# A linear-attention, routed-expert and gated-layer kernel: first routing group of four tiles, first expert's low halves on POOL, other steps per tile

## The chip, the core and the metric

The kernel runs on one NeuronCore of one Trainium2 chip. The metric is the device time of one execution, in microseconds. Three runs of the kernel before gave 971.5, 974.32 and 974.56 us, so its median is 974.32 us. The other rows and figures come from one further execution, taken with the hardware profiler.

## The reference

Three layers stand one behind the other, all in fp32, on 2304 tokens of width 512.

```
kv  = einsum('bhsd,bhse->bhde', k, v);  o = einsum('bhsd,bhde->bhse', q, kv)
x   = o / sqrt(mean(o*o) + 1e-6) * g_norm          # 4 batches, 8 heads, 576 x 64
l   = x @ w_gate + log1p(exp(x @ w_noise)) * noise # 8 experts, the two largest taken
out[mask] += weight * (maximum(x[mask] @ w1[e], 0) @ w2[e])   # 512 -> 1024 -> 512
y   = (1 / (1 + exp(-(out @ m2_gate))) * (out @ m2_val)) @ m2_out  # 512 -> 1536 -> 512
```

## The kernel before, in words

**Stages.** Attention works on 18 tiles of 128 tokens (`for t in range(NT)`, from L1307). Each tile is transposed (`q_transpose`: PE `pqT`, ACT `qT`), multiplied (`attend`: PE `po`) and read out by ACT in three instructions (`oraw`, `sq`, `Lr`), and DVE sums the squares (`ssq`). Between the tiles PE forms the products of keys and values of the next batch (`kv_a`, `kv_b`, `kv_c`: `pkv`, `pkvT`, `pgw`, and DVE's copies `kvbd`).

**Routing.** The tiles are routed in four groups (`GROUPS`). `route(g)` is a generator; each `yield` ends one step, and `advance(n)` moves all open groups n steps on. Its steps give, in this order: the norm (`rms_a`, `rms_y`), the normed logits (`Lr`, `lg`, `sp`, `nl`), the two largest experts (`m`, `oh`, `km`, `mk`), the rank of each token within its expert (PE's `prk` over `mk`, then `ohr`, `ri`, `sb`, `rm`), marks of the rank (`ohv`, L511: for group 0 all on POOL, for groups 1 and 2 half of them, for group 3 none) and the weights of the two experts. After groups 0 and 1, `list_first` makes PE sum the marks (`pfirst`); DVE writes the token numbers `lsa`, and POOL gathers the first two blocks of 128 rows for the first expert. After group 3 the same is done for all lists (`plist`, `lsb`), and POOL gathers the other three blocks.

**Experts.** A product is made in split precision: each operand is a high part and a low part, and three matmuls take high by high, low by high and high by low. `work()` splits one piece of a weight: a piece of `w1` (128x1024) is scaled by `gcol`, ACT writes the high half (L616) and DVE the low half (L617); for `w2` these are L619 and L620. Pieces of the last layer's weights pass through `work()` too. `scale` multiplies gathered rows by their norm (`xs`), `expert_in` transposes them on PE (`pxT`) and splits them (`xh` on ACT, `xl` on DVE). The first expert is done in two passes: `h_first(fp, 0)` for the 256 rows of the first two blocks, with fp = 0 to 3, 24 matmuls each, into `ha`; then `y_step` for the two blocks; then `h_first(fp, 1)` for the other 368 rows into `hh` and `hl`. In the trace `w_0h` to `w_3h` and `w_0l` to `w_3l` are the halves of piece fp; `w1` and `w2` carry the same names there.

**What sets the order.** SP and POOL issue in the order in which the program is written; ACT does so through attention and the first expert's first pass. PE and, until that pass, DVE are ordered by a scheduler that builds the program; where `in_order("DVE")` stands, DVE too keeps the written order. Within the first expert's second pass (L1400 on), the written order of each f is: `h_first` where f is odd, `pump` (splits of the next expert's weights), then POOL's gathers and scalings for expert 1 (L1415 to L1420).

## Time and profile before

| what | before |
|---|---|
| median of three runs | 974.32 us |
| lowest, highest | 971.5, 974.56 us |
| the profiled execution's own time | 973.39 us |
| its span in the trace | 971.6 us |
| PE busy | 930.7 us (96%) |
| DVE, ACT, POOL busy | 615.1, 420.2, 304.0 us |

The span runs from the first to the last instruction of the program; 1.8 us of the execution lie around it. PE's busy time is made of pipelined matmuls whose ends are modelled, so what PE waits for is read from the waits and the gaps and not from the 96%. All starts below count from the span's start.

### The profile page before, as it was taken

What the parts mean: (1) busy time and instruction counts of PE and PEld (TensorE: products, weight loads), DVE (VectorE), ACT (ScalarE), POOL (GpSimd) and SP (SyncE); (2) the same over time, 40 slices, a digit from 0 to 9 for tenths busy, and PEclk for the clock granted to TensorE, in tenths of its full rate; (3) what the DMA queues carried; (4) which work ended last, traced back from release to release, by engine and by line L of the source; (5) the groups of instructions that cost most, each with busy time, mean ns of one, the idle gap of its engine ahead of it and who ended that gap; (6) DMA issues with size and microseconds to landing.
All of it is one profiled execution on the core that took longest, in us unless ns stands there. A gap on an engine that the chain in (4) does not pass through costs nothing.

```text
span 971.6 us, 13989 instructions
## 1 busy us (share of the span) xinstructions
PE 930.7 (96%) x5207; PEld 811.4 (84%) x5207; DVE 615.1 (63%) x1017; ACT 420.2 (43%) x679; POOL 304.0 (31%) x299
## 2 busy tenths in 40 slices
PE   5997989999999999999999998999999999999998
PEld 5986779889898988989898897878788888888886
DVE  1398677858577585828732587676859888813221
ACT  1673443434343343333433676665655554403221
POOL 2141577171364728162201477760000000000000
PEclk8998999999999999999999999999999999999999
DMA  9984596868557465644701565655455747616451
GB/s 273 285 263 168 179 309 209 288 216 298 184 164 248 144 211 186 204 126 142 248 11 53 168 194 165 192 184 169 143 183 185 234 156 220 181 52 198 122 139 44
DMA packets 130441, 178.25 MB, mean 183 GB/s; under 512 B 18496, under 2 KB 76352, under 8 KB 130368
## 3 DMA queue, kind: packets, MB, share of 16 engines
q1 hardware_dynamic: 118608, 154.91, 49.7%
q0 software_dynamic: 8432, 20.26, 7.6%
q10 hardware_dynamic: 3328, 2.13, 0.7%
q8 instruction: 42, 0.69, 0.3%
q14 instruction: 31, 0.25, 0.1%
HBM read 123.12 MB, written 54.15 MB: 182 GB/s over the span
## 4 chain that ended last, share of the span: by engine, by line
PE 60%; DVE 6%; DMA 2%; ACT 2%; issue 2%; POOL 0%; ACTq 0%; DVEq 0%; POOLq 0%
PE pout L1252 15%; PE py L780 14%; PE pga L1154 11%; PE ph L736 10%; PE pgc L1154 6%; PE pgb L1154 3%; DMA raw<-in_moe_w_val_dram 1%; DVE hl L742 1%; DVE wt L978 1%; DVE xf L1052 1%; PE pgv L1122 1%; DMA yg<-ybuf,slot 1%; DVE raw L593 1%; DMA gbuf<-q 0%; DMA ybuf<-yo 0%
## 5 line engine op out<-in xcount | busy, mean ns | idle before, releaser
L677 POOL DMA_INDIRECT xg<-xbuf,lsq x132 | 141.1, 1069 | 149.0 <-DVE xT L723 100.4
L742 DVE SCALAR_TENSOR_TENSOR hl<-ph,hh 128x624 fp32r<-128x624 f32 (+1 forms) x60 | 48.7, 812 | 78.9 <-ACT hh L741 76.7
L741 ACT ACTIVATE hh<-ph 128x624 fp32r<-128x624 f32 (+1 forms) x60 | 41.7, 695 | 104.5 <-PE ph L736 99.4
L978 DVE TENSOR_TENSOR wt<-lw,wt 128x512 fp32r<-128x512 f32 x84 | 57.5, 687 | 31.8 <-ACT wt L977 31.6
L677 POOL DMA_INDIRECT yg<-ybuf,slq x64 | 69.3, 1083 | 19.5 <-issue 18.3
L785 ACT ACTIVATE yo<-py 128x512 f32<-128x512 f32 (+1 forms) x40 | 23.7, 593 | 72.3 <-PE py L780 48.4
L977 ACT ACTIVATE wt<-lw 128x512 fp32r<-128x512 f32 x84 | 50.4, 621 | 1.6 <-issue 1.6
L696 POOL TENSOR_TENSOR xg<-xg 128x512 f32<-128x512 f32 x33 | 37.7, 1145 | 39.8 <-DMA xg<-xbuf,lsq 34.5
L727 DVE TENSOR_TENSOR xl<-xT,xh 128x512 fp32r<-128x512 f32 (+3 forms) x40 | 24.8, 631 | 37.1 <-ACT xh L726 37.1
L1261 DVE COPY oo<-pout 128x512 f32<-128x512 f32 x9 | 6.2, 692 | 66.0 <-ACT oo L1263 53.1
L726 ACT ACTIVATE xh<-xT 128x512 fp32r<-128x512 f32 (+3 forms) x40 | 21.1, 543 | 53.3 <-DVE xT L723 53.3
L1168 ACT ACTIVATE q<-pga 128x1024 f32<-128x1024 f32 x24 | 24.6, 1025 | 42.1 <-PE pga L1154 39.1
L736 PE MATMUL ph<-xh,w_3h 128*128 128x312 f32 (+2 forms) x128 | 39.4, 308 | 3.5 <-DVE hl L742 3.5
L736 PE MATMUL ph<-xh,w_2h 128*128 128x312 f32 (+2 forms) x128 | 39.6, 310 | 3.3 <-DVE hl L742 3.3
L736 PE MATMUL ph<-xl,w_0h 128*128 128x312 f32 (+2 forms) x128 | 40.3, 315 | 1.8 <-DVE xl L727 1.8
L736 PE MATMUL ph<-xh,w_0h 128*128 128x312 f32 (+2 forms) x128 | 40.3, 315 | 0.7 <-ACT xh L726 0.6
L736 PE MATMUL ph<-xh,w_0l 128*128 128x312 f32 (+2 forms) x128 | 40.1, 313 | 0.3 <-PEq L815 0.3
L677 POOL DMA_INDIRECT yg<-ybuf,slot x20 | 19.6, 980 | 64.8 <-issue 53.9
L736 PE MATMUL ph<-xh,w_3l 128*128 128x312 f32 (+2 forms) x128 | 39.3, 307 | 0.0
L736 PE MATMUL ph<-xh,w_1h 128*128 128x312 f32 (+2 forms) x128 | 39.3, 307 | 0.0
L736 PE MATMUL ph<-xh,w_2l 128*128 128x312 f32 (+2 forms) x128 | 39.2, 306 | 0.1
L736 PE MATMUL ph<-xh,w_1l 128*128 128x312 f32 (+2 forms) x128 | 39.1, 306 | 0.0
(1260 smaller groups left out, 2978.8 us busy)
## 6 DMA issues: line engine op xcount, KB each, us to landing
raw<-in_moe_w_dram SPq DMA_DIRECT2D x60, 512.0 KB, 4.9
lw<-wbuf SPq DMA_DIRECT2D x84, 256.0 KB, 4.4
gr<-gbuf SPq DMA_DIRECT2D x18, 512.0 KB, 5.9
ybuf<-yo SPq DMA_DIRECT2D x32, 256.0 KB, 3.3
ybuf<-zero SPq DMA_DIRECT2D x29, 256.0 KB, 6.0
raw<-in_moe_w_gate_dram SPq DMA_DIRECT2D x12, 512.0 KB, 5.3
raw<-in_moe_w_val_dram SPq DMA_DIRECT2D x12, 512.0 KB, 4.6
gbuf<-qv SPq DMA_DIRECT2D x12, 512.0 KB, 3.1
```

What stands on the lines that cost most here:

```text
L677: nc.gpsimd.indirect_dma_start(out=x, out_offset=None, in_=src, in_offset=bass.IndirectOffsetOnAxis(ap=ix, axis=0))
L696: eng.tensor_mul(xv, xv, x[:, :, 128:, None].to_broadcast([128, 4, KD, 32]))
L727: nc.vector.tensor_sub(XL[e, s][:, :, a:z], pt[:, :, o:o + z - a], XA[e, s][:, :, a:z].bitcast(FT))
L736: nc.tensor.matmul(ph, w[:, c, j], x[e, s][:, c, :], start=(n == 0), stop=(n == 3 * KD - 1))
L741: nc.scalar.activation(hh, ph, AF.Relu)
L742: nc.vector.scalar_tensor_tensor(hl, ph, 0.0, hh.bitcast(FT), op0=OP.max, op1=OP.subtract)
L780: nc.tensor.matmul(py[0:m], x[:, f % 2, t], w[:, f % 2, :], start=(n == 0), stop=(n == 3 * FC - 1))
L977: nc.scalar.activation(hi, src, AF.Copy)
L978: nc.vector.tensor_sub(lo, src, hi.bitcast(FT))
L1154: nc.tensor.matmul(ps[:, j, 0:HT[c]], w[:, a, k, s], x[:, k, :], start=(first and i == 0), stop=(i == 5), skip_group_check=not first)
L1168: nc.scalar.activation(q[name], src, AF.Copy)
L1252: nc.tensor.matmul(po, g[x][1][:, f, :], w[:, k], start=(s + f + i == 0), stop=(s == 1 and FCUT + f == FC2 - 1 and i == 2))
```

## The change

It makes the first two routing groups four tiles each (before five and three), gives each tile its own number of routing steps (`STEPS`), and asks for the first lists right behind them. The four `raw` pieces of the first expert's `w1` are multiplied by `gcol` in place on POOL beside tiles 13 and 14, so that ACT's high half is a plain copy, and the low halves of these four and of two of the four `w2` pieces (1 and 3) are written by POOL. The first `w1` piece is split beside tile 15 and no other one inside attention. The first expert's first two blocks are scaled beside tile 16. The warming matmuls in front of the first pass go from four to two. In the second pass `h_first` comes at even f, ahead of that f's `pump`, and POOL scales expert 1's first two blocks ahead of the fourth and fifth block's gathers.

```diff
-GROUPS = [(0, 5), (5, 8), (8, 13), (13, 18)]
+GROUPS = [(0, 4), (4, 8), (8, 13), (13, 18)]
...
-FIRST_SPLIT = 16
+FIRST_SPLIT = 15
+
+STEPS = {3: 6, 4: 4, 5: 4, 6: 3, 7: 3, 8: 3, 9: 3, 10: 3, 11: 3, 12: 3, 13: 3}
...
             if u[0] == "w1":
-                nc.scalar.activation(hi, raw, AF.Copy, scale=gcol)
-                nc.vector.scalar_tensor_tensor(lo, raw, gcol, hi.bitcast(FT), op0=OP.mult, op1=OP.subtract)
+                if u[1]:
+                    nc.scalar.activation(hi, raw, AF.Copy, scale=gcol)
+                    nc.vector.scalar_tensor_tensor(lo, raw, gcol, hi.bitcast(FT), op0=OP.mult, op1=OP.subtract)
+                else:
+                    nc.scalar.activation(hi, raw, AF.Copy)
+                    nc.gpsimd.tensor_sub(lo, raw, hi.bitcast(FT))
             else:
                 nc.scalar.activation(hi, raw, AF.Copy)
-                nc.vector.tensor_sub(lo, raw, hi.bitcast(FT))
+                eng = nc.vector if u[1] or u[2] % 2 == 0 else nc.gpsimd
+                eng.tensor_sub(lo, raw, hi.bitcast(FT))
...
-        advance(1)
         g = group_of[t]
         if t == groups[g][1] - 1:
             routes.append((g, route(g)))
-        if t >= FIRST_SPLIT:
+        advance(STEPS.get(t, 2) - 1)
+        list_first()
+        if FIRST_SPLIT - 2 <= t < FIRST_SPLIT:
+            for x, _ in list(raws)[:2] if t == FIRST_SPLIT - 2 else list(raws)[2:]:
+                nc.gpsimd.tensor_scalar(x, x, gcol, None, op0=OP.mult)
+        if t == FIRST_SPLIT:
             work()
-        list_first()
+        if t == NT - 2:
+            with tc.high_priority():
+                for blk in range(AB):
+                    scale(0, blk, nc.vector)
 
     pw = pa([128, HP * 128], "warm")
-    for _ in range(4):
+    for _ in range(2):
...
-    while not XG:
-        advance(1)
-        list_first()
-    advance(2)
     with in_order("DVE"):
         with tc.high_priority():
             for blk in range(AB):
-                scale(0, blk, nc.vector)
-        advance(1)
-        with tc.high_priority():
-            for blk in range(AB):
                 expert_in(0, blk)
+        work()
         advance(4)
...
-            elif f % 2:
+            elif f % 2 == 0:
                 h_first(f // 2, 1)
...
-                for blk in range(NB - 1) if f == 0 else ():
+                for blk in range(NB - 2) if f == 0 else ():
                     gather(1, blk)
-                if f > 2:
-                    scale(1, f - 3, nc.gpsimd)
+                if f == 1:
+                    scale(1, 0, nc.gpsimd)
+                    scale(1, 1, nc.gpsimd)
+                    gather(1, NB - 2)
+                if f in (3, 5, 7):
+                    scale(1, f // 2 + 1, nc.gpsimd)
```

In the following rows lines count in each kernel's own file, `x4` means four alike in a row, and a name as `w_0_1l` is a weight of expert 0, piece 1, low half (in the trace `w_1l`).

PE in attention, beside tiles 5 to 7. Before, from the transposes of batch 2's products (`pkvT`) on:

```order
L347 MATMUL pkvT<-ident,kvbd_232 128x128 x4
L378 MATMUL pqT<-ident,qp 128x128 x4
L393 MATMUL po<-kvbd_230,qT 128x160 x4
L354 MATMUL pgw<-early,kvT 128x32 x4
L378 MATMUL pqT<-ident,qrem 128x128 x4
L393 MATMUL po<-kvbd_230,qT 128x160 x4
```

With the change, from the product of tile 6 on:

```order
L395 MATMUL po<-kvbd_230,qT 128x160 x4
L471 LDWEIGHTS tri
L471 MATMUL prk<-mk,tri 128x32
L473 LDWEIGHTS ones
L473 MATMUL prk<-mk,ones 128x24
L473 LDWEIGHTS ones
L473 MATMUL prk<-mk,ones 128x16
L473 LDWEIGHTS ones
L473 MATMUL prk<-mk,ones 128x8
L477 LDWEIGHTS ones
L477 MATMUL prk<-before,ones 128x32
L380 MATMUL pqT<-ident,qp 128x128 x4
```

The ranks of group 0 now stand behind tile 6 and ahead of tile 7's transposes; before, they stood behind the transposes of batch 3 (`kvbd_234`), beside tile 11.

ACT at attention's end. Before:

```order
L444 ACTIVATE sp<-lg 128x40
L445 ACTIVATE sp<-sp 128x40
L616 ACTIVATE w_0_0h<-raw,gcol 128x1024
L396 ACTIVATE oraw<-po 128x4x4x32
L399 ACTIVATE sq<-po 128x512
L400 ACTIVATE Lr<-po 128x128
```

With the change:

```order
L446 ACTIVATE sp<-lg 128x40
L447 ACTIVATE sp<-sp 128x40
L398 ACTIVATE oraw<-po 128x4x4x32
L401 ACTIVATE sq<-po 128x512
L402 ACTIVATE Lr<-po 128x128
L622 ACTIVATE w_0_0h<-raw 128x1024
L382 ACTIVATE qT<-pqT 128x512
L398 ACTIVATE oraw<-po 128x4x4x32
L401 ACTIVATE sq<-po 128x512
L402 ACTIVATE Lr<-po 128x128
```

The first weight's high half stood ahead of tile 17's read-out; it now stands ahead of tile 17's `qT` and of the read-outs of tiles 16 and 17.

POOL, from the first marks to expert 1's gathers. Before:

```order
L511 TENSOR_SCALAR ohv<-i_204,rm 128x128 x13
L677 DMA xg<-xbuf,lsa 128x528 x2
L511 TENSOR_SCALAR ohv<-i_204,rm 128x128 x5
L677 DMA xg<-xbuf,lsb 128x528 x5
L677 DMA xg<-xbuf,lsq 128x132 x8
L800 MEMSET zero 128x512
L683 TENSOR_TENSOR xs_0_1641<-xg 128x4x4x32
L677 DMA xg<-xbuf,lsq 128x132 x4
L683 TENSOR_TENSOR xs_1_1655<-xg 128x4x4x32
```

With the change:

```order
L684 DMA xg<-xbuf,lsa 128x528 x2
L1333 TENSOR_SCALAR raw<-raw,gcol 128x1024 x4
L623 TENSOR_TENSOR w_0_0l<-raw,w_0_0h 128x1024
L623 TENSOR_TENSOR w_0_1l<-raw,w_0_1h 128x1024
L513 TENSOR_SCALAR ohv<-i_204,rm 128x128 x5
L623 TENSOR_TENSOR w_0_2l<-raw,w_0_2h 128x1024
L623 TENSOR_TENSOR w_0_3l<-raw,w_0_3h 128x1024
L627 TENSOR_TENSOR w_0_1l<-raw,w_0_1h 128x1024
L627 TENSOR_TENSOR w_0_3l<-raw,w_0_3h 128x1024
L684 DMA xg<-xbuf,lsb 128x528 x5
L684 DMA xg<-xbuf,lsq 128x132 x4
L690 TENSOR_TENSOR xs_0_1592<-xg 128x4x4x32
```

Four scalings and six subtractions now lie between the two sets of gathers, and `xs_0` (with `xs_1` right behind it) comes after four quarter gathers, where it came after eight and `xs_1` after twelve.

The first expert's second pass, DVE. Before:

```order
L617 SCALAR_TENSOR_TENSOR w_1_0l<-raw,gcol,w_1_0h 128x1024
L617 SCALAR_TENSOR_TENSOR w_1_1l<-raw,gcol,w_1_1h 128x1024
L742 SCALAR_TENSOR_TENSOR hl_0_1555<-ph,hh_0_1554 128x2x368
L617 SCALAR_TENSOR_TENSOR w_1_2l<-raw,gcol,w_1_2h 128x1024
L617 SCALAR_TENSOR_TENSOR w_1_3l<-raw,gcol,w_1_3h 128x1024
L620 TENSOR_TENSOR w_1_0l<-raw,w_1_0h 128x1024
L742 SCALAR_TENSOR_TENSOR hl_1_1606<-ph,hh_1_1605 128x2x368
```

With the change:

```order
L749 SCALAR_TENSOR_TENSOR hl_0_1531<-ph,hh_0_1530 128x2x368
L620 SCALAR_TENSOR_TENSOR w_1_0l<-raw,gcol,w_1_0h 128x1024
L620 SCALAR_TENSOR_TENSOR w_1_1l<-raw,gcol,w_1_1h 128x1024
L620 SCALAR_TENSOR_TENSOR w_1_2l<-raw,gcol,w_1_2h 128x1024
L620 SCALAR_TENSOR_TENSOR w_1_3l<-raw,gcol,w_1_3h 128x1024
L749 SCALAR_TENSOR_TENSOR hl_1_1602<-ph,hh_1_1601 128x2x368
```

`hl_0` moved ahead of two weight pieces, `hl_1` ahead of one. On PE, with the change, behind the third piece's matmuls (before, `pxT` stood behind the fourth piece's):

```order
L726 MATMUL pxT<-ident,xs_0_1592 128x128 x4
L726 MATMUL pxT<-ident,xs_1_1594 128x128 x2
L787 MATMUL py<-w_0_0h,hh_0_1530 128x512
L726 MATMUL pxT<-ident,xs_1_1594 128x128
L787 MATMUL py<-w_0_0l,hh_0_1530 128x512
L726 MATMUL pxT<-ident,xs_1_1594 128x128
L787 MATMUL py<-w_0_0h,hl_0_1531 128x512
L787 MATMUL py<-w_0_0h,hh_0_1530 128x512
L743 MATMUL ph<-xh_1_1468,w_0_3h 128x368
L743 MATMUL ph<-xl_1_1469,w_0_3h 128x368
```

Expert 1's first transposes and the first four matmuls of an output block now stand ahead of the fourth piece.

## Rows read from the trace of the kernel before

**Rows 1.** Stretch: us; PE, PEld, DVE, ACT, POOL busy (instructions); PEclk, DMA share, GB/s.

```profile
62.00:82.60 20.60, 12.90 (x91) 9.74 (x91) 18.39 (x78) 12.24 (x31) 7.71 (x11) 0.94 0.53 180
82.60:96.70 14.10, 14.04 (x102) 13.67 (x103) 12.52 (x49) 5.37 (x10) 4.28 (x5) 0.84 0.44 157
112.00:134.20 22.20, 17.22 (x98) 16.01 (x98) 16.14 (x30) 12.30 (x14) 17.44 (x16) 1.00 0.89 287
134.20:153.10 18.90, 18.90 (x80) 15.13 (x81) 14.77 (x19) 6.20 (x11) 13.04 (x13) 0.91 0.77 254
180.00:971.00 791.00, 777.21 (x3997) 672.88 (x3995) 495.13 (x693) 339.04 (x526) 228.82 (x214) 1.00 0.54 171
```

**Rows 2.** PE's waits, 75 to 175 us: total us, times, longest.

```profile
PE prk L469 <- DVE mk L464: 3.5, 1, 3.5
...
PE ph L736 <- DVE xl L727: 1.8, 2, 1.5
```

**Rows 3.** PE's waits, 112 to 135 us.

```profile
PE ph L736 <- DVE hl L742: 2.6, 2, 1.4
PE pxT L719 <- POOL xs L683: 2.0, 1, 2.0
```

**Rows 4.** Timeline in attention: start us, us, engine line op out<-in.

```profile
39.61 0.86 DVE L340 COPY kvbd<-pkv 64x256 f32<-64x256 f32 x2 [3.14 <-PE pkv L337]
...
43.42 1.25 PE L393 MATMUL po<-kvbd,qT 128*128 128x160 f32 x8
...
44.90 0.58 ACT L380 ACTIVATE qT<-pqT 128x512 f32<-128x512 f32 x1
...
46.19 0.20 DVE L428 TENSOR_TENSOR rms_y<-rms_u,rms_y 128x40 f32<-128x40 f32 x1
...
46.48 0.62 ACT L380 ACTIVATE qT<-pqT 128x512 f32<-128x512 f32 x1
...
55.81 0.19 DVE L464 TENSOR_TENSOR mk<-oh 128x40 bf16<-128x40 f32 x1
...
67.86 0.16 DVE L1298 TENSOR_SCALAR lsa<-pfirst 128x2 int32<-128x2 f32 x1 [0.22 <-PE pfirst L1289]
...
72.03 1.13 ACT L616 ACTIVATE w_0h<-raw,gcol 128x1024 fp32r<-128x1024 f32 x1
...
74.03 0.28 ACT L400 ACTIVATE Lr<-po 128x128 f32<-128x128 f32 x1
```

**Rows 5.** Timeline of the first expert's first pass, its input and its end.

```profile
79.11 1.08 ACT L726 ACTIVATE xh<-pxT 128x512 fp32r<-128x512 f32 x2 [3.19 <-PE pxT L719]
...
81.25 1.28 DVE L727 TENSOR_TENSOR xl<-pxT,xh 128x512 fp32r<-128x512 f32 x2
...
82.59 0.58 PE L736 MATMUL ph<-xl,w_0h 128*128 128x256 f32 x1 [1.54 <-DVE xl L727]
...
96.67 0.63 PE L780 MATMUL py<-w_0h,ha 128*128 128x512 f32 x2
```

**Rows 6.** POOL's groups by shape: busy us, mean ns, idle before.

```profile
L511 POOL TENSOR_SCALAR ohv<-i,rm 128x128 f16<-128x128 f16 x18 | 13.4, 762 | 28.4 <-DVE rm L502 16.1 <-DVE oraw L431 12.3
...
L368 POOL COPY qp<-q 128x1024 f32<-128x1024 f32 x6 | 6.2, 1040 | 30.5 <-DMA q<-in_q_dram 29.6 <-PE po L393 0.9
...
L683 POOL TENSOR_TENSOR xs<-xg 128x512 f32<-128x512 f32 x2 | 2.1, 1061 | 0.0
```

**Rows 7.** Timeline: POOL's gathers, and the second pass's first matmul.

```profile
68.31 1.18 POOL L677 DMA_INDIRECT xg<-xbuf,lsa  x1 [0.73 <-DVE oraw L431]
...
100.97 1.76 POOL L677 DMA_INDIRECT xg<-xbuf,lsb  x1 [13.61 <-DVE lsb L1357]
...
112.07 0.43 PE L736 MATMUL ph<-xh,w_0h 128*128 128x368 f32 x1
```

**Rows 8.** The same columns as group 1, behind the wait of 2.0 us.

```profile
134.00:138.00 4.00, 3.81 (x14) 3.09 (x15) 4.00 (x4) 1.19 (x2) 2.14 (x3) 0.61 0.95 325
```

**Rows 9.** DVE's line 617, first piece: ns shortest/median/longest, first and last start.

```profile
L617 DVE SCALAR_TENSOR_TENSOR w_0l<-raw,gcol,w_0h x8: 1277/1280/2389, 73.3 to 469.7; 128x1024 fp32r<-128x1024 f32 x8
```

## The prediction

> **What bounds the kernel now.** I read the table of stages first, then PE's waits, then the timeline where PE waits, since only there can the change give anything. Behind 180 us PE is busy 777 of 791 us [rows 1]: what PE starts earlier there ends earlier, and nothing in that stretch is edited. The gaps lie ahead of it: between 62 and 82.6 us PE is busy 12.9 of 20.6 us, and between 112 and 134.2 us 17.2 of 22.2 [rows 1]. The first is the hand-over from attention to the first expert: PE waits 3.5 us for `mk` of group 2, which stands on DVE behind two weight pieces and two scalings, and 1.8 us for `xl` [rows 2]. The second is the first expert's second pass: 2.6 us for `hl`, 2.0 us for `xs` on POOL [rows 3]. So the sum has three terms: when the first pass starts, how much of that is left when the second pass starts, and how long the second pass takes.
>
> **First pass's start.** Before, it starts in earnest at 82.59 us, with `xl`; attention's last read-out starts at 74.03 and ends at 74.3 [rows 4, 5].
>
> *Attention's end.* Smaller groups let group 0 begin some five microseconds sooner, but the order puts its ranks on PE behind tile 6, which PE has done at 43.42+1.25 = 44.7 us [rows 4]. `mk` must be there first. DVE copies batch 2's `kvbd` ahead of group 0's `rms_y`, and that copy ends at 39.61+0.86 = 40.5 us, bound by PE [rows 4]. From `rms_y` to `mk` group 0 took 55.81+0.19-46.19 = 9.8 us before, mixed with group 1's steps [rows 4]; its own share I put at 5.4, so `mk` comes at 45.9 and PE waits 1.2 us. ACT's next `qT` copies what PE transposes behind that wait, and so comes as late; I carry 2 us into tiles 8 to 12. Bounds: nothing, and 40.5+9.8-44.7 = 5.6 us.
> Group 1 has four tiles instead of three, so its marks are no sooner by much: `lsa` at 66.9 instead of 67.86 [rows 4]. What it queues is new: on DVE group 2's norm stands behind `lsa`, and on ACT tile 14's `qT` behind that norm's `rms_y`, which gets there at 67.7. From there ACT's list is a sum. A tile costs 46.48-44.90 = 1.58 us [rows 4], so four tiles 6.3; `sp` with its wait 0.9; the first weight's high half, now ahead of tile 17, 1.13 [rows 4]; and tile 17's own wait for its product, which follows its `qT`, about 1.2. That is 9.5 us, so attention ends at 77.3, 3 us later than before.
>
> *From there.* The two scalings of rows are on DVE ahead of attention's last sums, so done by 76.3, and the two weight pieces (1.28 us each, [rows 9]) are gone from DVE. What remains is `xh` 1.08 and `xl`, of which one half, 0.64, lies behind the second `xh` [rows 5], and about 0.5 of sums: 77.3+1.1+1.2 = 79.6 us. **The first pass starts 3.0 us earlier.** The bounds are 0 and 6.
>
> **First pass's end: POOL's new queue.** It took 96.67-82.59 = 14.1 us [rows 5]. POOL now supplies the low halves. The nearest rows for a subtraction of 128x1024 are its 128x512 products at 1.06 us, so 2.1 [rows 6]. No row has a scaling of 128x1024: below stands the copy of that size, 1.04, above the marks' rate, 0.76 us for 128 elements and 6.1 for 1024 [rows 6]. I take 1.5: the copy has the same elements and type and is the nearer, and I add what a mark costs beyond 128 elements at the copy's rate, most of it fixed. Both ends go into the range.
> POOL's list: gathers from 66.9, issued by 69.6 (as 68.31 to 70.8 before, [rows 7]); four scalings to 75.6; `w_0l` to 77.7, in time. `w_1l` waits for ACT's `w_1h`, which follows `xh`: 78.4+1.1 = 79.5, so `w_1l` at 81.6; five marks of 0.76 to 85.4; `w_2l` 87.5; `w_3l` 89.6. PE wants `w_2l` at about 87.5 and `w_3l` at 90. So POOL fits with nothing to spare, and the pass ends at 79.6+14.1 = 93.7, or 93.9 with slips, 2.8 us earlier.
>
> **Second pass's start.** POOL is now late for another reason: its five gathers stand behind two more subtractions, of `w2` pieces 1 and 3, and these wait for ACT, which writes `w_1h` only after the last `ha`: 93.9+0.6+1.1 = 95.5. Two subtractions end at 99.7, and the gathers start there instead of at 100.97 [rows 7]. The second pass follows its gathers by 112.07-100.97 = 11.1 us as before. **Left of the 3 us: 1.3.** DVE, freed of two pieces, has `lsb` ready by 98 to 99, so it does not decide.
>
> **The second pass.** `hl_0` no longer stands behind two weight pieces and `hl_1` behind one fewer; and PE has eight transposes and four output matmuls, about 1.8 us, to do between pieces 2 and 3 while `hl_1` is written. So both waits for `hl`, 2.6 us, go [rows 3]. `xs_0` and `xs_1` come after four quarter gathers instead of eight and twelve, so some 13 us sooner by the issue of POOL; the wait of 2.0 us goes too [rows 3]. Right behind that wait the granted clock is 0.61 of full speed over 4 us [rows 8], between the levels of 1.2 and 2.4 GHz; PE had been idle 2 us. Without the wait 4x0.39 = 1.6 us come back. Together 6.2 us. Against it: new short waits of DVE beside POOL, 0.4; and expert 1's last rows, which DVE and ACT must have split some 6 us sooner than before while DVE is busy 14.8 of 18.9 us [rows 1]: 0.5. **5.3 us.** The bounds are 2.6, if only the `hl` waits go, and 6.2.
>
> **Sum.** 1.3+5.3 = 6.6 us. Two fewer warming matmuls cost nothing and give nothing; PE is idle there. Against the profiled execution's 973.4 us (span 971.6 and 1.8 around it) that is 966.8; the median of the three runs is 0.9 above that execution. I forecast **967.2 us**.
>
> **Rivals**, each 0.4 above the sum against the profiled execution, as the forecast is.
> *(a) Attention ends as early as before.* For it: the wait for `mk` on PE rests on an estimate, and the chain behind `lsa` too. Then the pass starts near 76.6, and POOL binds: `w_1l` at 79.8, `w_3l` 87.8, the pass's end 91.5, the gathers 97.5, 3.5 us earlier instead of 1.3: 965.0.
> *(b) POOL and DVE slow each other.* One of line 617's pieces took 2.39 us where the median is 1.28 [rows 9], with POOL's products of 128x512 beside it. The change puts 6.0+12.6+3.8 = 22.4 us of POOL into a stretch in which DVE, busy 12.5 of 14.1 us [rows 1], routes groups 2 and 3. If a fifth is added to POOL's work, 4.5 us, the first pass ends 3 us later than I say, the gathers start at 104, and the loss of 3.2 us leaves 5.3-3.2 = 2.1 us: 971.7. The Trainium skill says the same (GPSIMD Engine Reference, Specifications): GPSIMD's SBUF interfaces are shared with VectorE and contended by DVE instructions with two SBUF inputs. By that rule nearly all of these subtractions would be hit; the one row here bears it out for DVE, and POOL's own products kept close to 1.06.
> *(c) The second pass keeps a wait.* The next expert's weights land late, or `hl_1` still comes after PE: 3 us of the 5.3 stay, 970.2.
> *(d) Slower: POOL's scaling runs at the marks' rate.* Four at 6.1 us end at 94 instead of 75.6; ACT's high half waits for the first, PE's third matmul for `w_0l` at 96, 14 us after its time before; the gathers come at 115. That costs 14.0-5.3 = 8.7 us: 982.5. At 4 us each the gathers come at 106.6, and the loss of 5.6 less 5.3 leaves 974.1: it decides from about 3.9 us a scaling. Against it stand POOL's copy and products, which keep to one or two ns an element; for it, only the marks. The Trainium skill holds a one-input operation on GPSIMD to be roughly at line rate (GPSIMD Engine Reference, Engine selection), which speaks against (d); no row here shows this form.
>
> **Chances.** My forecast 0.42, (a) 0.20, (b) 0.17, (c) 0.13, (d) 0.08. About 0.3%, 2.9 us, is what a measurement of this kernel can tell from no change, so faster means under 971.4 and slower over 977.2. Faster: 0.42+0.20, two thirds of (c) and under half of (b), 0.77. Slower: most of (d) and the tail of (b), 0.07. The rest, 0.16, is no change. The range reaches from 961, a little under what (a) gives with the second pass at its bound and a scaling at the copy's 1.04 (965.0-0.9-1.8 = 962.3), to 974.5, which takes in (b), (c) and the half-way case of (d).
>
> **What the changed profile would show.** Right: PE waiting for `mk` of group 0 near 45 us; ACT's last `Lr` near 77; the first pass's `xl` matmul near 80 and the first output matmul near 94; POOL busy without a break from the gathers to `w_3l` and again up to the second gathers at about 100; no PE wait for `hl` or `xs` in the second pass, and the clock at 1.00 behind it; expert 1 some 7 us earlier than before. Wrong: scalings of over 2 us or subtractions of over 2.6; PE waiting for low halves from POOL for more than 2 us; a second pass that starts no earlier, or still has its gap.

## The result and the profile after

The changed kernel took **984.18 us** (median of 983.37, 983.93, 984.43 and 990.22) against 972.91 us for the kernel before (median of four): the ratio is 1.0129, with a 95% interval of 1.0083 to 1.0175. Forecast were 967.2 us, within 961.0 to 974.5. The profiled execution took 983.37 us, with a span of 981.6.

The same stretches as [rows 1], after (the last one is longer by the 10 us of the span):

```profile
62.00:82.60 20.60, 11.49 (x98) 9.49 (x97) 18.67 (x60) 10.85 (x28) 16.57 (x11) 0.86 0.39 130
82.60:96.70 14.10, 12.02 (x69) 9.95 (x69) 9.86 (x26) 5.30 (x10) 6.77 (x7) 0.72 0.20 61
112.00:134.20 22.20, 17.54 (x90) 14.55 (x90) 12.81 (x31) 3.50 (x6) 11.98 (x10) 0.85 0.45 138
134.20:153.10 18.90, 18.90 (x109) 17.82 (x108) 16.56 (x13) 13.10 (x15) 16.17 (x15) 1.00 0.83 262
180.00:981.00 801.00, 786.12 (x4066) 681.52 (x4065) 506.68 (x709) 342.81 (x530) 233.32 (x218) 1.00 0.54 172
```

POOL is busy 16.57 us in the first stretch where it was 7.71, and PE loses 1.4 there. PE's waits from 75 to 175 us, against [rows 2, 3]:

```profile
PE prk L471 <- DVE ssq L407: 6.0, 1, 6.0
PE po L395 <- ACT qT L382: 3.6, 1, 3.6
PE plist L1296 <- DVE ohv L517: 2.5, 1, 2.5
PE ph L743 <- DVE ha L749: 2.1, 1, 2.1
PE py L787 <- POOL w_1l L627: 1.3, 1, 1.3
PE ph L743 <- POOL w_3l L623: 0.6, 1, 0.6
...
PE ph L743 <- POOL w_2l L623: 0.2, 1, 0.2
```

All of these lie in the hand-over; the second pass has no wait for `hl` or `xs` left. The last three are waits for low halves from POOL, 2.1 us together. The timeline of PE at the steps on which the sum rested:

```profile
77.64 0.90 PE L395 MATMUL po<-kvbd,qT 128*128 128x160 f32 x2 [3.62 <-ACT qT L382]
84.51 0.19 PE L471 MATMUL prk<-mk,tri 128*128 128x40 bf16 x1 [5.97 <-DVE ssq L407]
...
91.48 0.38 PE L743 MATMUL ph<-xl,w_0h 128*128 128x256 f32 x1 [0.17 <-DVE xl L734]
...
109.16 0.40 PE L787 MATMUL py<-w_0h,ha 128*128 128x512 f32 x1
...
129.85 0.43 PE L743 MATMUL ph<-xh,w_0h 128*128 128x368 f32 x1
...
163.86 0.30 PE L743 MATMUL ph<-xh,w_0h 128*128 128x312 f32 x1
```

Tile 17's product stops after two matmuls: group 2's ranks stand in the middle of it and wait for `mk`. (The profile puts that wait down to a sum of squares, `ssq`, whose record ends together with that of `mk`, at 84.44 us; the ranks read `mk`.) The first pass starts 8.9 us late (82.59 before, [rows 5]), its first output product comes 12.5 us late, the second pass 17.8 us late ([rows 7]). The second pass then takes 34.0 us where it took 41.0, so expert 1's first product is 10.8 us late (153.05 before). From there to the end it is 817.7 us after and 818.6 before: what lies behind it took 0.9 us less.

**Why `mk` was late.** POOL's scalings as a group (ns shortest/median/longest), and then its timeline:

```profile
L1333 POOL TENSOR_SCALAR raw<-raw,gcol x4: 2832/2833/2864, 70.8 to 79.3; 128x1024 f32<-128x1024 f32 x4
```

```profile
76.44 5.65 POOL L1333 TENSOR_SCALAR raw<-raw,gcol 128x1024 f32<-128x1024 f32 x2
...
79.26 2.83 POOL L1333 TENSOR_SCALAR raw<-raw,gcol 128x1024 f32<-128x1024 f32 x1
...
82.07 2.33 POOL L623 TENSOR_TENSOR w_0l<-raw,w_0h 128x1024 fp32r<-128x1024 f32 x1
91.73 2.40 POOL L623 TENSOR_TENSOR w_1l<-raw,w_1h 128x1024 fp32r<-128x1024 f32 x1 [7.33 <-ACT w_1h L622]
...
102.96 2.40 POOL L623 TENSOR_TENSOR w_3l<-raw,w_3h 128x1024 fp32r<-128x1024 f32 x1 [2.83 <-ACT w_3h L622]
111.08 2.36 POOL L627 TENSOR_TENSOR w_1l<-raw,w_1h 128x1024 fp32r<-128x1024 f32 x1 [5.71 <-ACT w_1h L625]
...
117.51 1.78 POOL L684 DMA_INDIRECT xg<-xbuf,lsb  x1 [1.75 <-DVE lsb L1364]
```

(The first of these rows covers the third and the fourth scaling, the second the fourth alone.) And DVE's, only instructions that last far longer than their like elsewhere (0.31 us for the three copies `oraw`, 0.24 for `oh`, 0.17 for `ee`, 0.19 for `mk`, 0.16 for `dn` and `tw`):

```profile
70.06 1.95 DVE L433 COPY oraw<-rms_y 128x16 f32<-128x16 f32 x3
...
75.99 1.65 DVE L458 TENSOR_TENSOR oh<-nl,m 128x80 f32<-128x80 f32 x1
...
78.69 1.77 DVE L464 TENSOR_TENSOR oh<-keys,km 128x80 f32<-128x80 f32 x1
80.38 4.04 DVE L481 TENSOR_SCALAR ee<-km 128x5 f32<-128x5 f32 x1
...
80.53 3.91 DVE L466 TENSOR_TENSOR mk<-oh 128x40 bf16<-128x40 f32 x1
...
103.06 2.34 DVE L524 TENSOR_TENSOR dn<-m 128x5 f32<-128x5 f32 x1
...
111.13 2.33 DVE L530 TENSOR_TENSOR tw<-tw,dn 128x5 f32<-128x5 f32 x1
```

Add start and length. `mk` ends at 84.44, the subtraction beside it at 84.40; `dn` at 105.40, its subtraction at 105.36; `tw` at 113.46, its subtraction at 113.44. Beside the scalings it is different: the first `oh` ends at 77.64 and the second at 80.46, each 1.20 us into a scaling of 2.83; both had started half a microsecond ahead of that scaling, beside the end of the one before. And `mk` stood beside both: it starts at 80.53, while the last scaling runs, 1.5 us before the subtraction does. Six records that start between 80.38 and 81.84 (two `ee`, `mk`, two `xs`, one `ssq`) all end at 84.42 to 84.45. DVE's trivial instructions wait for POOL's long ones, and the profile counts them as busy: DVE shows 18.67 us of work in a stretch of 20.6 in which part of that was standing still.

### The profile page after: what moved, and what is told of

It is laid out like the page before. It is cut to its first block, busy times and chain, and to the rows that moved or that the text cites. A ratio compares the mean times of both kernels' runs of the same rounds, so it can differ in the third digit from the quotient of the medians.

```text
span 981.6 us, 13993 instructions
## 1 busy us (share of the span) xinstructions
PE 931.5 (95%) x5203; PEld 812.0 (83%) x5203; DVE 628.5 (64%) x1012; ACT 419.7 (43%) x679; POOL 326.1 (33%) x308
## 4 chain that ended last, share of the span: by engine, by line
PE 59%; DVE 6%; DMA 2%; ACT 2%; issue 1%; POOL 0%; ACTq 0%; DVEq 0%; POOLq 0%
PE pout L1259 15%; PE py L787 14%; PE pga L1161 11%; PE ph L743 10%; PE pgc L1161 6%; PE pgb L1161 3%; DMA raw<-in_moe_w_val_dram 1%; DVE hl L749 1%; DVE wt L985 1%; DVE xf L1059 1%; PE pgv L1129 1%; DMA yg<-ybuf,slot 1%; DVE raw L595 0%; DMA ybuf<-yo 0%; DMA gbuf<-q 0%
## 5 line engine op out<-in xcount | busy, mean ns | idle before, releaser
L743 PE MATMUL ph<-xl,w_2h 128*128 128x312 f32 (+2 forms) x128 | 39.8, 311 | 0.0
```

Source lines behind the costliest of these rows:

```text
L743: nc.tensor.matmul(ph, w[:, c, j], x[e, s][:, c, :], start=(n == 0), stop=(n == 3 * KD - 1))
```

## The experiments

Expert 1's first product is the yardstick: from it to the end it is 817.6 to 819.3 us in eleven traces, of both kernels and nine trials, and 820.2 and 821.4 in two more. Four kernels (`w1` unscaled, the two that part groups and attention's end, the long idle scalings) ran on a chip where the kernel before took 1027 us. What that chip added shows behind expert 1's first product, from which it is 871.5 to 879.7 us to the end. Ahead of it the two kernels with attention's new end and the old groups, one on that chip and one on another, have their first `xl` product at the same 79.12 us. So these traces are compared up to expert 1.

| kernel | attention's last `Lr` ends | first `xl` product | second gathers | expert 1 | time, ratio to before |
|---|---|---|---|---|---|
| before | 74.3 | 82.6 | 101.0 | 153.1 | 1 |
| changed | 88.0 | 91.5 | 117.5 | 163.9 | 1.0129 [1.0083, 1.0175] |
| second pass alone | 74.1 | 83.3 | 101.9 | 147.0 | 0.9942 [0.9922, 0.9962] |
| and new groups | 78.5 | 86.2 | 103.1 | 149.6 | 1.0011 [0.9963, 1.0058] |
| and new end of attention | 74.0 | 79.1 | 103.5 | 150.4 | 1.0013 [0.9969, 1.0057] |
| all but POOL's part | 79.3 | 84.5 | 107.9 | 153.6 | 1.0014 [0.9994, 1.0034] |
| with `w2` 1, 3 on POOL | 79.4 | 83.7 | 112.2 | 155.0 | 1.0026 [1.0009, 1.0043] |
| with `w1` too, unscaled | 81.7 | 84.9 | 110.9 | 156.8 | 1.0064 [1.0015, 1.0114] |
| changed, in quarters | 82.4 | 85.7 | 120.3 | 163.1 | 1.0084 [1.0060, 1.0108] |

So the parts, taken in the order of the table and each from one trace, come at expert 1 to this: the second pass gives 6.1 us; the groups cost 2.6, attention's end 3.4, both together 6.6; the two `w2` pieces on POOL 1.4, the four `w1` pieces 1.8, the scalings 7.1. Their sum is +10.8.

### Taking the change apart

**The second pass alone**, on the kernel before:

```diff
-            elif f % 2:
+            elif f % 2 == 0:
                 h_first(f // 2, 1)
...
-                if f > 2:
-                    scale(1, f - 3, nc.gpsimd)
+                if f == 1:
+                    scale(1, 0, nc.gpsimd)
+                    scale(1, 1, nc.gpsimd)
+                    gather(1, NB - 2)
+                if f in (3, 5, 7):
+                    scale(1, f // 2 + 1, nc.gpsimd)
```

> The kernel before with nothing but the new order of the second pass: the matmuls of a piece at even f, ahead of that f's splits, and POOL's scalings behind four quarter gathers. Theory A (the reorder is worth by itself what the changed kernel shows between its second pass's first matmul and expert 1, 33.3 us instead of 41.0): 5 to 8 us faster than before, near 966 us, with no wait of PE for hl or xs behind 112 us. Rival (in the changed kernel the second pass came 18 us later, so that its gathers, weights and rows had that much more time; by itself the reorder brings little): under 3 us faster, with a wait of PE for rows or weights in place of the old ones.

968.0 us, 0.9942 of before. PE's waits from 112 to 175 us, and the stretch of [rows 1]:

```profile
PE ph L736 <- DVE hl L742: 0.6, 2, 0.4
PE pcnt L1380 <- DVE xl L727: 0.3, 1, 0.3
```

```profile
112.00:134.20 22.20, 21.57 (x130) 20.35 (x129) 18.74 (x31) 13.17 (x16) 16.74 (x16) 1.00 0.85 270
```

Theory A: PE is busy 21.57 us of 22.2 where it was 17.22. Only 0.6 us of waits for `hl` are left, where theory A had none. This kernel beats both; run once more beside later ones it took 967.1 us, 0.9935 [0.9912, 0.9957], expert 1 at 147.1.

> The kernel with the new second pass alone once more, beside the others on the same chip, so that the kernel with one split less is measured against it. Both theories: 0.991 to 0.997 of before, expert 1's first product within 0.7 us of 147.0.

**All but POOL's part.**

```diff
-                if u[1]:
-                    nc.scalar.activation(hi, raw, AF.Copy, scale=gcol)
-                    nc.vector.scalar_tensor_tensor(lo, raw, gcol, hi.bitcast(FT), op0=OP.mult, op1=OP.subtract)
-                else:
-                    nc.scalar.activation(hi, raw, AF.Copy)
-                    nc.gpsimd.tensor_sub(lo, raw, hi.bitcast(FT))
+                nc.scalar.activation(hi, raw, AF.Copy, scale=gcol)
+                nc.vector.scalar_tensor_tensor(lo, raw, gcol, hi.bitcast(FT), op0=OP.mult, op1=OP.subtract)
...
-                eng = nc.vector if u[1] or u[2] % 2 == 0 else nc.gpsimd
+                eng = nc.vector
...
-                nc.gpsimd.tensor_scalar(x, x, gcol, None, op0=OP.mult)
```

> The changed kernel with all of the first expert's low halves back on DVE and no scaling on POOL; grouping, steps, the first split beside tile 15, the rows scaled beside tile 16 and the second pass stay as changed. Theory A (POOL's long instructions hold up DVE's small ones, and that is what made attention end 13.6 us later): attention's last Lr is back at 74 to 78 us, the first pass's xl matmul at 80 to 83, the gathers at 99 to 102, and the time 963 to 968 us. Rival B (the new order holds it up by itself: group 2's ranks stand ahead of tile 17's product on PE, the rows' scalings ahead of the ranks on DVE): attention's last Lr stays behind 82 us and the time is 972 us or more.

974.1 us. DVE's long instructions are gone and attention ends 8.7 us sooner than in the changed kernel: theory A there. But it ends at 79.3, not by 78, the first pass starts at 84.5, not by 83, the gathers at 107.9, not by 102, and the time is rival B's: at expert 1, 6.6 of the 16.9 us that separate the changed kernel from the second pass alone have nothing to do with POOL.

**With `w2` pieces 1 and 3 on POOL**, against the kernel just shown:

```diff
-                eng = nc.vector
+                eng = nc.vector if u[1] or u[2] % 2 == 0 else nc.gpsimd
```

> As the kernel without POOL's low halves and scalings, but w2's pieces 1 and 3 still get their low halves on POOL. Theory A (an instruction of POOL holds up DVE for as long as it lasts, and PE's list of marks waits for DVE): the two subtractions, 2.36 us each, stand where DVE writes the last marks, so the gathers come 3 to 5 us later than without them, and the time is 2 to 4 us above that kernel's, 966 to 971 us. Rival (these two pieces are only moved off DVE): 1 to 2.5 us below that kernel, because DVE has two pieces of 1.22 us less.

The gathers come 4.3 us later, as theory A said, and expert 1 1.4 us. The time, 1.7 us more, is below its 2 to 4, and the two intervals overlap; the gain of the rival is not there.

**The changed kernel without the scalings** (the first expert's `w1` unscaled).

```diff
-        if FIRST_SPLIT - 2 <= t < FIRST_SPLIT:
-            for x, _ in list(raws)[:2] if t == FIRST_SPLIT - 2 else list(raws)[2:]:
-                nc.gpsimd.tensor_scalar(x, x, gcol, None, op0=OP.mult)
```

> The changed kernel without the four scalings on POOL; the order on the other engines is the same, and POOL still writes all six low halves. It leaves out the multiplication of the first expert's w1 by gcol. Theory A (the scalings, 11.3 us of POOL beside group 2's routing, are what delayed attention's end): attention's last Lr falls from 87.7 to 78 to 81 us, the first pass starts 6 to 8 us earlier, and the time is 975 to 979 us: the 6 us of the order and 2 to 4 us for the subtractions remain. Rival B (the subtractions hold up as much, the scalings only came first): the time stays at 980 us or more.

Attention ends 6.2 us sooner, the first pass starts 6.6 us sooner and expert 1 7.1 us: theory A, whose bound for the start of `Lr`, 81, is missed by 0.4; its forecast of the time can't be tested on that chip. Scalings that nothing waits for cost only 2.1 us (below). Why they cost 7.1 here is read from rows, without a run of its own. `w_0l` stands 6.5 us earlier on POOL's list in this run, and holds an instruction of the same chain all the same; POOL's row, then DVE's:

```profile
75.53 2.35 POOL L623 TENSOR_TENSOR w_0l<-raw,w_0h 128x1024 fp32r<-128x1024 f32 x1 [4.86 <-issue]
```

```profile
75.58 2.40 DVE L464 TENSOR_TENSOR oh<-keys,km 128x80 f32<-128x80 f32 x1
```

That the scalings put `w_0l` back until it meets `mk` does not explain it, then. `mk` ends at 78.23 here and at 84.44 in the changed kernel, 6.2 us apart. Up to there DVE's instructions last 2.2 us longer than their like in this run, all in this `oh`, and 8.3 us in the changed kernel: 1.6 in the copies `oraw`, 1.4 and 1.5 in the two `oh`, 3.7 in `mk`. Beside the idle scalings below, the short instructions ahead of `mk` grew by 1.4 us in all, and POOL took 13.35 us for the four instead of 11.31: there DVE's long instructions ran at the same time, and by the lengths POOL did part of the waiting.

**Groups and attention's end apart**, each on the second pass alone. The first takes the groups and steps:

```diff
-GROUPS = [(0, 5), (5, 8), (8, 13), (13, 18)]
+GROUPS = [(0, 4), (4, 8), (8, 13), (13, 18)]
+STEPS = {3: 6, 4: 4, 5: 4, 6: 3, 7: 3, 8: 3, 9: 3, 10: 3, 11: 3, 12: 3, 13: 3}
...
-        advance(1)
...
+        advance(STEPS.get(t, 2) - 1)
```

The second takes the rest of attention's end (two warming matmuls, and these lines). Both ask for the lists ahead of `work`, so the two are not quite the halves of one edit.

```diff
-FIRST_SPLIT = 16
+FIRST_SPLIT = 15
...
-        if t >= FIRST_SPLIT:
+        if t == FIRST_SPLIT:
             work()
+        if t == NT - 2:
+            with tc.high_priority():
+                for blk in range(AB):
+                    scale(0, blk, nc.vector)
...
-    advance(2)
...
+        work()
         advance(4)
```

> The kernel before with the new groups and steps a tile and the new second pass, and attention's end, the splits and the start of the first pass as before. The kernel with everything but POOL's part took 974.1 us, that with the second pass alone 968.0. Theory C (the 6 us between them come from attention's end: in the first pass ACT's dn and sp, which wait for group 2's late routing on DVE, stand ahead of ha): 966 to 970 us here, with the first pass's first output product at 96 to 98 us. Rival D (they come from the groups: group 1's four tiles and fewer steps a tile put all of group 2's routing back): 971 us or more, with the first pass as late as in that kernel, and the loss is not in the sibling that changes attention's end alone.

> The counterpart: the kernel before with the new second pass and the new end of attention (one split beside tile 15, the rows scaled beside tile 16, two warming matmuls, the second split behind the first pass's input), but groups and steps as before. Theory C (attention's end loses the 6 us): 971 us or more. Rival D (the groups lose them): 966 to 970 us. If both kernels lose, 970 to 972 us each.

At expert 1 both lose against the second pass alone, 2.6 and 3.4 us. The times, 1.0011 and 1.0013 of before, say the same, with intervals that lie just above that of the second pass alone and room for the 970 to 972 us (0.9965 to 0.9986 of before) that were expected if both lose. With the old groups the first pass starts at 79.1, as early as forecast, and then takes 19.3 us.

### What POOL does to DVE

**Idle work on POOL**, on the kernel before: sixteen short scalings, four long ones, four long subtractions.

```diff
+        if XG and not done:
+            done.append(t)
+            x = raws[-1][0]
+            for _ in range(4):
+                nc.gpsimd.tensor_sub(x, x, once[:, :, None].to_broadcast([128, KD, 256]))
```

(`once` is zero here; with scalings the last line is `tensor_scalar(x, x, once, None, op0=OP.mult)` with ones, and for the short ones sixteen scalings of a tile of their own.)

> The kernel before with 16 scalings of a 128x256 tile that nothing else reads or writes, on POOL right behind the first two gathers, where POOL sat idle for 12 us; no data of the kernel waits for them. The output is the same. Theory A (DVE's instructions that read or write through what POOL uses wait until POOL's instruction ends): small DVE instructions between 71 and 83 us take up to 1 us more each, mk of group 2 comes 2 to 8 us later, and the time rises by 1.5 to 8 us. Rival B (POOL and DVE work side by side, and what was late in the changed kernel were data): no DVE instruction gets longer, and the time is within 0.3% of before.

> The kernel before with four more instructions on POOL behind the first two gathers: each multiplies the fourth raw piece of w1 (128x1024) by 1.0 in place, the form of the changed kernel's scalings. The piece is not read before 90 us, so nothing waits for them, and the output is the same. Theory A (an instruction of POOL holds DVE up for as long as it lasts, so four of 2.8 us hurt where sixteen of 1.1 us cost a few tenths each): some DVE instructions between 71 and 84 us last 1 to 4 us where they took 0.2, mk of group 2 starts behind 81 us instead of at 78.2, and the time rises by 2.5 to 8 us. Rival B (DVE and POOL share a rate, and length doesn't matter): DVE's instructions grow by tenths as beside the 128x256 ones, and the time rises by less than 1.5 us.

> As the kernel with four idle scalings of 128x1024, but each of the four is a subtraction of zero with two operands, the form of the changed kernel's low halves. The piece is not read before 90 us, nothing waits for them, and the output is the same. Theory A (a subtraction on POOL holds up a DVE instruction until it ends, 2.33 us, where a scaling holds it up for its first 1.2 us): between 71 and 81 us at least two DVE instructions end within 0.1 us of the end of a subtraction, mk of group 2 starts behind 80 us (79.4 beside the scalings), and expert 1's first product comes at 155.5 us or later (155.2). Rival B (both forms hold DVE up alike): mk of group 2 near 79.4 us and expert 1 near 155.2 us or sooner.

Scalings: theory A failed, and so, by a few tenths, did the short ones' rival B, since `w_1l` took 1.50 us beside them instead of 1.28. Short or long, they put `mk` of group 2 1.0 and 1.2 us back (78.17 before) and expert 1 2.2 and 2.1 us; the times, 1.0004 [0.9989, 1.0019] and 0.9995 [0.9950, 1.0040], show nothing. The long ones come near their rival B: three of DVE's short instructions grew by 0.25 to 0.83 us. The scalings themselves grew, from 2.83 us up to 3.78, while DVE's two splits and two scalings beside them kept their lengths:

```profile
L1334 POOL TENSOR_SCALAR raw<-raw,once x4: 2842/3222/3780, 70.5 to 81.0; 128x1024 f32<-128x1024 f32 x4
```

Subtractions: theory A held. `mk` 5.0 us late, expert 1 4.1 us, time 980.05 us, 1.0067 [1.0044, 1.0090], for 7.8 us of work on an idle engine that no data waits for. The subtractions, then DVE beside them:

```profile
L1334 POOL TENSOR_TENSOR raw<-raw,once x4: 1892/1893/1901, 70.4 to 76.3; 128x1024 f32<-128x1024 f32 x4
```

```profile
71.15 1.20 DVE L532 TENSOR_TENSOR tw<-tw,dn 128x3 f32<-128x3 f32 x1
72.27 0.67 DVE L409 TENSOR_REDUCE ssq<-sq 128x8 f32<-128x512 f32 x1
72.86 1.48 DVE L451 TENSOR_TENSOR sp<-sp,early 128x40 f32<-128x40 f32 x1
74.38 1.94 DVE L453 TENSOR_TENSOR nl<-lg,sp 128x40 f32<-128x40 f32 x1
76.35 0.44 DVE L456 MAX8 m<-nl 128x8 f32<-128x8 f32 x5
76.82 1.50 DVE L460 TENSOR_TENSOR oh<-nl,m 128x80 f32<-128x80 f32 x1
```

The subtractions end at 72.31, 74.28, 76.25 and 78.22; `tw`, `sp`, `nl` and `oh` end at 72.35, 74.34, 76.32 and 78.32. The reduction and the MAX8 between them last what they always last. They read one tensor, but that alone is not the reason: in the changed kernel copies (`oraw`, 1.95 us) and scalings by a scalar (two marks `ohv`, 2.52 us beside `w_1l`), which read one tensor too, were held.

**The changed kernel with POOL's scalings and subtractions cut into quarters** of 128x256.

```diff
-                    nc.gpsimd.tensor_sub(lo, raw, hi.bitcast(FT))
+                    for i in range(KD):
+                        nc.gpsimd.tensor_sub(lo[:, i], raw[:, i], hi.bitcast(FT)[:, i])
```

> The changed kernel with every scaling and subtraction on POOL cut into four of 128x256, the same work in the same place. Theory A (length is what hurts: a short instruction holds DVE up for a few tenths, and DVE gets in between): no DVE instruction between 68 and 118 us is held up for more than 1 us, against up to 4 us; but sixteen scalings take 1.1 us each instead of 0.7, so POOL is busy with them for 18 us instead of 11.3, and the first low half comes behind 89 us. The two about cancel: attention's last Lr ends at 80 to 84 us instead of 87.9, and expert 1's first product comes at 158 to 165 us (163.9 uncut). Rival B (the same bytes through the same place cost the same): attention's last Lr at 87 us or later.

982.8 us. Attention's end and expert 1 came as theory A said, its first claim failed: behind one another, eight quarters hold one DVE instruction, which starts 1.0 us ahead of them and ends 0.2 us behind the last. And PE waited 4.0 us for `w_0l` itself, since sixteen short scalings took 16.0 us and put it back to 92.1. POOL's timeline, then DVE's:

```profile
89.33 2.78 POOL L624 TENSOR_TENSOR w_0l<-raw,w_0h 128x256 fp32r<-128x256 f32 x4
92.07 2.79 POOL L624 TENSOR_TENSOR w_1l<-raw,w_1h 128x256 fp32r<-128x256 f32 x4
```

```profile
88.36 6.72 DVE L427 TENSOR_TENSOR rms_u<-rms_y 128x40 f32<-128x40 f32 x1
```

### What is not POOL's

On the kernel with all but POOL's part: once without the two warming matmuls, once with group 3's `sp` behind the second `ha`. Then the latter on the kernel with attention's new end and the old groups.

```diff
-    for _ in range(2):
-        nc.tensor.matmul(pw, qT[NT - 1][:, 0], qT[NT - 1].rearrange("p h d -> p (h d)"), start=True, stop=True)
```

```diff
         if fp < 3:
             work()
-        advance(4)
+        advance((2, 6, 4, 4)[fp])
```

> The kernel without POOL's low halves and scalings (974.1 us, expert 1's first product at 153.6), and without its two warming matmuls, which there run from 79.3 to 81.2 us, between group 2's ranks and the first expert's transposes. Theory E (with attention's end put together anew they lie on the path): the transposes start at about 79.3 us, the first pass's xl product at 82.6 to 83 instead of 84.5, and expert 1's first product 1 to 2 us earlier. Rival F (the first pass waits for DVE later anyway, or a lower clock takes back what is saved): expert 1's first product within 0.5 us of 153.6.

> The same kernel with group 3's softplus (sp) put behind the first pass's second ha on ACT, and the routing steps behind it as much later; the number of steps is the same. In that kernel ACT's second ha stood behind sp, which waited for lg on DVE, and PE then sat 2.2 us in the middle of the pass. Theory E (the order on ACT costs that wait): the wait is gone, the first output product comes at 99 to 100.5 us instead of 101.8, expert 1's first product 0.5 to 2 us earlier. Rival F (DVE is full from 68 us to its last mark, so the second gathers come when DVE is through, whatever PE does): the first output product comes earlier, but the second gathers stay within 0.7 us of 107.9 and expert 1 within 0.7 us of 153.6.

> The kernel with the new second pass and the new end of attention on the old groups, whose first pass started at 79.1 us but took 19.3 us, with sp behind the third piece's ha as in the sibling. Theory E: the first output product at 94 to 96.5 us instead of 98.4, expert 1's first product at 145 to 148.5 us instead of 150.4, and so near the 147.0 of the new second pass alone or below it. Rival F: the second gathers at 102.5 us or later, expert 1 at 149.5 us or later.

Without the matmuls the transposes start 2.5 us earlier and `xl` at 82.05 instead of 84.48, but the granted clock is then 0.50 (1.2 of 2.4 GHz) from 82 to 86 us, where it was 0.78 with them, and expert 1 comes at 152.9 instead of 153.6: they lay on the path, and the clock took nearly all back: at the second piece, without a wait between, the lead of 2.4 us has fallen to 0.4. That is nearer rival F, whose 0.5 us it misses by 0.2, than theory E; the time shows no gain (975.4 us, 1.0028 [1.0007, 1.0049], against 1.0014).

DVE's and then ACT's timeline of the kernel with all but POOL's part show the order that held PE up for 2.2 us there, `ha` behind `sp`, and `sp` behind `dn`:

```profile
93.50 0.16 DVE L524 TENSOR_TENSOR dn<-m 128x5 f32<-128x5 f32 x1
```

```profile
93.69 0.21 ACT L526 ACTIVATE dn<-dn 128x5 f32<-128x5 f32 x1 [4.51 <-DVE dn L524]
93.80 0.22 ACT L446 ACTIVATE sp<-lg 128x40 f32<-128x40 f32 x1
94.06 0.24 ACT L447 ACTIVATE sp<-sp 128x40 f32<-128x40 f32 x1
94.20 0.58 ACT L744 ACTIVATE ha<-ph 128x512 fp32r<-128x512 f32 x1
```

With `sp` later `dn` still stands ahead of `ha`, and PE still waits 1.7 us there (ACT's row, then PE's):

```profile
93.23 0.21 ACT L526 ACTIVATE dn<-dn 128x5 f32<-128x5 f32 x1 [4.51 <-DVE dn L524]
```

```profile
95.01 0.39 PE L739 MATMUL ph<-xh,w_3h 128*128 128x256 f32 x1 [1.73 <-ACT w_3h L618]
```

The first output product comes at 100.6 instead of 101.8, but the gathers come at 110.1 and expert 1 at 155.0, 2.2 and 1.4 us later than without. So the wait that theory E wanted gone stayed, and rival F's bounds, 0.7 us, were passed on the late side (978.0 us, 1.0032 [1.0002, 1.0061]).

On the old groups the first output product came at 92.5, better than forecast, the gathers at 99.0 and expert 1 at 147.2, with 969.1 us, 0.9950 [0.9934, 0.9967]: theory E, 3.1 us better at expert 1 than the same kernel with `sp` where it was (on another chip), but no gain on the second pass alone. From the gathers to the second pass's first product, 112.9, PE is busy there for 13.4 of 13.9 us, at a granted clock of 0.65 from 99 to 103 us: in this run PE and its clock set that start, and no longer DVE.

**One split less ahead of the first pass**, on the second pass alone:

```diff
-FIRST_SPLIT = 16
+FIRST_SPLIT = 17
...
                 expert_in(0, blk)
+        work()
         advance(4)
```

> The kernel with the new second pass alone, and the first expert's second piece split behind the first pass's input instead of ahead of it. DVE has 1.3 us less ahead of the scaled rows and of mk of group 2. Theory A (DVE's list is what the first pass's start waits for): xl's first product at 81.5 to 82.5 us instead of 83.3, expert 1's first product at 145.5 to 146.7 us instead of 147.0, the time 0.3 to 1.5 us below that of the second pass alone. Rival B (DVE is full until the last marks, so what starts earlier waits later): expert 1's first product at 147 us or later, the time as that kernel's or above.

`xl` at 82.1, but the gathers at 104.2 and expert 1 at 150.0; 970.4 us, 0.9963 [0.9950, 0.9976]: rival B. None of the runs that moved PE's start forward came out ahead of the second pass alone.

## Why the prediction was wrong, by its steps

The sum had two terms at expert 1. The second pass's start, forecast 1.3 us earlier, came 17.8 later; the second pass, forecast 5.3 us shorter, was 7.0 shorter. So the first term failed, and within it two steps: POOL's new work was priced by when POOL delivers, as if it cost DVE nothing ahead of the second pass, where it cost 10.3 us at expert 1; and the new groups and attention's end were entered as a gain of 3.0 us, where they cost 6.6 us without any of POOL's part.

- **Where the bound is.** Right for the second pass, wrong for the hand-over. I read PE's waits there as the order on DVE and took DVE's time as free to be rearranged; DVE, busy 12.5 of 14.1 us [rows 1], set the second gathers. Of the trials that let PE start sooner, three found the gathers later or within 0.5 us of where they were; only the one on the old groups with `sp` later had them sooner, and there the time went to PE.
- **Attention's end**, forecast 77.3: 79.3 without POOL's part, 88.0 with it. `mk` of group 0 came at 47.1 instead of 45.9, PE waited 0.8 for it instead of 1.2, `lsa` came at 67.9 instead of 66.9. These were near, and the 2.0 us are a miss of this term's own. The 8.7 us on top are the step that failed: the POOL list was checked for being in time (`w_0l` "in time" at 77.7), never for what it does to its neighbour.
- **From attention's end to the first pass**, forecast 2.3 us: 3.5, and 5.2 without POOL's part. There ranks and a warming matmul stand ahead of the eight transposes, and these take 1.9 us at a granted clock of 0.50, the level of 1.2 GHz, where they took 1.1 before at 1.00; PE had been busy 1.9 of the 4.0 us from 74 to 78.
- **POOL's prices.** A subtraction took 2.33 to 2.40 (2.1 forecast), a scaling 2.83 (1.5, bounds 1.04 and 6.1), 2.7 times the copy that I had taken as the nearest row. Four scalings put `w_0l` at 84.4 us instead of 77.7. By rival (d)'s own sum that delay alone would not have turned the sign, which it does from 3.9 us a scaling. As far as the rows show, what the scalings cost is DVE's standing still beside them: without them attention ends 6.2 us sooner and expert 1 comes 7.1 us sooner. Of the signs that I had named for a wrong forecast, scalings of over 2 us and PE's waits of over 2 us for POOL's low halves (2.1) came; subtractions of over 2.6 us did not.
- **The first pass's length**, 14.1 forecast: 17.7, and 17.3 without POOL's part, where `ha` behind `dn` and `sp` held PE 2.2 us. I carried the length over from a pass that had started later beside the same routing on DVE. That was a term of its own.
- **"Two fewer warming matmuls cost nothing"** held only in outcome. They moved onto the path (79.3 to 81.2 us), and leaving them out gained 0.7 us at expert 1 and nothing in the time, because the clock takes it back.
- **The second pass**, forecast 5.3, bounds 2.6 and 6.2: 7.0 (41.0 to 34.0 us). The mechanism was right. PE's idle time in it fell from 4.9 to 0.3 us, the 4.6 of the waits of [rows 3], its busy time from 36.1 to 33.7. Of that, 1.6 is what I had put for the clock [rows 8]: its mean over the pass was 0.96 before and is 1.00 after. Where the other 0.8 comes from is open. The 0.9 that I took off for new waits never came.
- **Rival (b)** named the mechanism, and its size was wrong. I added a fifth to POOL's work; in fact DVE stood still for as long as a subtraction lasted. The row that I cited showed a hold already: the piece of 2.39 us, 1.11 more than its like, starts at 134.84 beside two POOL products that run from 134.07 to 136.13. The Trainium skill states this elsewhere than I looked (SBUF — State Buffer, Who interferes with whom): DVE and GPSIMD share one pair of ports under an exclusive lock that is held for a whole instruction, and which of the two issues first decides who waits. The same section counts in DVE's instructions with two inputs in SBUF, and copies and scalings by a scalar where they run in a two-port mode, and leaves reductions out. The four idle subtractions agree to within 0.1 us, and so does a held mark in the changed kernel (`ohv`, 2.36 us from 91.83, beside `w_1l`, which ends at 94.13). The scalings do not: two instructions of DVE got through 1.2 us into a scaling of 2.83, and `mk` began to wait 1.5 us before the subtraction that it ended with. By that rule the six subtractions, an estimate of 12.6 us by my own price, would have stood in the sum as time taken from DVE, against the 7.6 us of its own pieces that it was freed of, and the first two terms could hardly have been gains.
- **Rival (c)**'s sum was wrong: 970.2 us is what comes out if 3 of the 5.3 us are lost; if 3 stay, as it says, it is 969.5. Nothing in the outcome rests on it.
- **Faster, 0.77**, stood on one term, the second pass, which alone does give 0.9942. The loss came from parts that I had entered as gains.

What stays open: why two instructions of DVE wait 1.2 us into a scaling and no longer, which of POOL's instructions held `mk` for its first 1.5 us, and how the 6.6 us of groups and attention's end split further; they interlock through DVE.

## What to carry to other kernels

An idle POOL is not a free engine. Before moving work there, list what DVE does at that time: if those are short instructions with two operands in SBUF, copies or scalar operations on a chain to the critical engine, each long two-operand instruction on POOL stops them until it ends, and cutting it up does not help while the pieces follow one another. Scalings on POOL, which stopped them for part of their time, cost the most here, 7.1 of POOL's 10.3 us. And when several edits come in one change, price each by its own stage: here the second pass, which had nothing to do with the others, was worth 6 us and the rest cost 17.

## What was not expected of the hardware

- On POOL a scaling of 128x1024 by a scalar per partition (one tensor operand, 2.83 us) costs more than a subtraction of two tensors of that size (2.33 to 2.40), and a subtraction of one broadcast column costs 1.89. The copy takes 1.04 [rows 6]. Scalings of 128x256 take 1.0 to 1.1 each, 16.0 and 18.3 us for the sixteen.
- By the lengths the hold works both ways: beside DVE's splits of 1.28 us the four long idle scalings took 13.35 us instead of 11.31, one of them 3.78.
- DVE's reductions, MAX8 and `ha` (an operand in PSUM, 0.68 us at 98.65 beside a subtraction of 97.78 to 100.13) kept their times, but for one `ssq` behind held instructions: its record, 2.60 us from 81.84, ends together with theirs.
